# A squared-relu attention with a gated two-layer product behind it: shared PSUM pairs, av in bursts of a quad, visits of three items

## The chip, the cores and the metric

The kernel runs on one NeuronCore of a Trainium2 chip. The engines that matter are TensorE (PE in the profile; its weight loads are PEld), VectorE (DVE), ScalarE (ACT), GpSimd (POOL) and SyncE (SP, whose queue here issues DMAs). Each engine takes its instructions in the order in which the program lists them, and waits on semaphores for others. The metric is the device time of one execution in microseconds; the kernel before took 425.79 us (median of 3 runs, 425.36 to 425.98).

## The reference

Eight batches, 12 heads, 448 positions, 64 values a head. Attention without softmax: the scores are cut at zero and squared. The heads' outputs, side by side, are 3584 tokens of 768 values, which go through a 768 x 2048 product, a sigmoid-gated activation and a 2048 x 768 product.

```python
def _attn_ref(q, k, v):
    S = q.shape[2]
    scores = (1.0 / np.sqrt(q.shape[-1])) * np.matmul(q, k.transpose(0, 1, 3, 2))
    attn = np.maximum(scores, 0.0) ** 2 / S
    return np.matmul(attn, v)

def _moe_ref(x, w_in, w_out):
    h = x @ w_in
    g = h * (1.0 / (1.0 + np.exp(-1.702 * h)))
    return g @ w_out

x = attn_out.transpose(0, 2, 1, 3).reshape(B * S, H * D)
out = _moe_ref(x, w_in, w_out)
```

## The kernel before

**Attention.** The work unit is a quad: four heads of one batch, so three quads a batch and 24 in all (`units`, number u). A quad's 448 positions are cut into J = 7 slots of 64 keys. For a slot, `scores` (L145) runs four 64x64 matmuls side by side in the array, each 448 wide, into one PSUM pair `sc` (two banks). `relu2` then makes `rl` from it with a relu (ACT, L159; for slot 3 of the quads of batch 1 DVE, L156) and squares it on DVE into `at` (L160). `av_mm` (L170) multiplies a slot's `at` with v and adds it to the quad's PSUM pair `av` over the seven slots. `xt_evac` (L187) copies a finished `av` on DVE into `xt`, the transposed tokens of a group.

**The two products.** The tokens are cut into NG = 8 groups of 6 or 8 blocks of 64, so 384 or 512 tokens by turns. `m1(g, f)` (L226) makes 128 of the 2048 middle values for a group: six matmuls into the PSUM tile `ht`, then gelu on ACT (L231, `gf`), then scaling to fp16 on POOL (L233, `gt`). One such call is called an ht group here. `m2(g, m, h)` (L244) makes half of the output columns for 128 tokens: 16 matmuls into `op`, an eviction by DVE (L249, `osb`), and with the second half two stores on SP (L255). This is an op group. `ht`, `op` and the PE transposes `tr` share one pool of two PSUM tiles, `ps_m`.

**PSUM and buffers.** `ps_s` has two pairs for `sc`, `ps_v` one pair for `av`. There are three `rl`, six `at` and five v buffers.

**The order.** It is written out by hand. `visit(n)` takes the next n slots: it issues their scores, then the av of the slots that earlier visits left in `pend` (up to the end of a quad), the xt copy where a quad is finished, and last the relus and squares of the new slots. Batch 0 runs alone in visits of two; PE transposes (`trans_pe`, L128, copied out by ACT at L133 or DVE at L135) make kT and qT for quads 0 to 5. Then the 16 ht groups of group 0 run, with visits for batch 1 between them. Quads 6 and up are loaded in fp32 by SP (`load_qk`, L80), cast by DVE (k) and POOL (q) at L102, and transposed by DMA on SP's queue (`trans`, L109). Their first loads stand in SP's queue behind `sp_gate` (L273), a tiny transfer that reads a w_out block and so waits for it. From group 1 on, a list `moe` mixes the ht groups of g with the op groups of g-1. Each adds its estimated time to `acc`, and when that passes a due time tv, a visit follows. If a group's first ht needs quads that aren't finished, visits are forced.

**Loads and weights.** POOL's queue issues the loads that cast to fp16: k, q (`load16`, L117) and v (`load_v`, L89), and the weights, w_in in four blocks of two transfers (`w1`, L262) and w_out in four blocks (`w2`, L267). Two w_in blocks are triggered at the start, the others and w_out from `pool_work`, each behind the ht group of that number, and so behind that group's `gt` in POOL's queue.

Of the kernel before, what the change touches and what calls it, by code (L numbers as in the profile page):

```python
# [15 lines left out]
def kernel(  # L16
# [9 lines left out]
    nc = tc.nc  # L26
# [26 lines left out]
    atp = ctx.enter_context(tc.tile_pool(name="atp", bufs=6))  # L53
# [4 lines left out]
    ps_s = ctx.enter_context(tc.tile_pool(name="ps_s", bufs=2, space=bass.MemoryType.PSUM))  # L58
    ps_v = ctx.enter_context(tc.tile_pool(name="ps_v", bufs=1, space=bass.MemoryType.PSUM))
# [133 lines left out]
    slots = [(u, j) for u in range(NU) for j in range(J)]  # L193
    pend = []
# [3 lines left out]
    def visit(n):  # L198
        new = slots[pos[0]:pos[0] + n]
        pos[0] += len(new)  # L200
        scs = [scores(u, j) for u, j in new]
        ready = []
        while pend:
            ready.append(pend.pop(0))
            if ready[-1][1] == J - 1:
                break
        for u, j, at in ready:
            av_mm(u, j, at)
        if ready and ready[-1][1] == J - 1:
            xt_evac(ready[-1][0])  # L210
            done_units[0] = ready[-1][0] + 1
        for (u, j), sc in zip(new, scs):
            pend.append((u, j, relu2(u, j, sc)))
# [23 lines left out]

    def m2(g, m, h):
        if h == 0:
            osb[g, m] = osp.tile([128, DM], F32, name="osb", tag="osb")  # L240
        ot = osb[g, m]
        op = ps_m.tile([128, 512], F32, name="op", tag="mm")
        for f in range(NF):
            nc.tensor.matmul(  # L244
                out=op[:, 0:NOUT],
                lhsT=gts[g][:, f, m * 128:(m + 1) * 128],
                rhs=wout[h][f // WO][:, f % WO, :],
                start=(f == 0), stop=(f == NF - 1))
        nc.vector.tensor_scalar(out=ot[:, h * NOUT:(h + 1) * NOUT], in0=op[:, 0:NOUT],  # L249
                                scalar1=1.0 / SC, scalar2=None, op0=ALU.mult)  # L250
        if h == 1:
            for i in range(2):
                b, j = divmod(gcum[g] + 2 * m + i, J)
                r0 = b * S + j
                nc.sync.dma_start(out=out[r0:r0 + 63 * J + 1:J, :],  # L255
                                  in_=ot[64 * i:64 * i + 64, :])
# [34 lines left out]
    with tc.manual_schedule():  # L291
# [20 lines left out]
        trans_pe(0, "q", 4)  # L312
        n = 0
        while pos[0] < NP * J:
# [5 lines left out]
            if n == 5:  # L320
                trans_pe(2, "k", 0)
                trans_pe(2, "q", J)
            if n == 9:
                load16(4, "k")
                load16(4, "q")
            if n == 10:
# [18 lines left out]
        while pend:  # L345
            visit(0)
# [20 lines left out]
        def step_visit(n):  # L367
            visit(n)
            if pos[0] < len(slots):
                u = slots[pos[0]][0]  # L370
# [72 lines left out]
```

## Time and profile before

| | |
|---|---|
| timed runs | 425.79 us (425.36 to 425.98) |
| profiled execution | 424.03 us, its span 422.3 us |
| granted TensorE clock | 0.991 (mean) |
| busy in the span | TensorE 93%, ACT 49%, DVE 45%, POOL 31% |
| loads on POOL's queue | k 6, q 6 and v 24 of 224 KB; w_in 8 of 384 KB; w_out 4 of 768 KB (sizes as they land) |
| loads and stores on SP's queue | k 18 and q 18 of 448 KB; 56 stores of 192 KB |

The span is that of the profiled execution, from its first instruction to its last; the execution's own time is a little more. A row of the chain or the timeline reads: start, duration, engine, line, operation, output<-input, count, and in brackets the idle time before it with what ended it. A row of waits reads: who waited <- for whom: us in total, times, the longest. A row of the stage table gives the length of a stage, the busy time of each engine with its number of instructions, the granted clock, the share of 16 DMA engines that was asked for, and GB/s. A row of DMA issues ends with KB each and the median us to landing, or with the latter alone.

### The profile page before, as it was taken

What the parts mean: (1) busy time and instruction counts of PE and PEld (TensorE: products, weight loads), DVE (VectorE), ACT (ScalarE), POOL (GpSimd) and SP (SyncE); (2) the same over time, 40 slices, a digit from 0 to 9 for tenths busy, and PEclk for the clock granted to TensorE, in tenths of its full rate; (3) what the DMA queues carried; (4) which work ended last, traced back from release to release, by engine and by line L of the source; (5) the groups of instructions that cost most, each with busy time, mean ns of one, the idle gap of its engine ahead of it and who ended that gap; (6) DMA issues with size and microseconds to landing.
All of it is one profiled execution on the core that took longest, in us unless ns stands there. A gap on an engine that the chain in (4) does not pass through costs nothing.

```text
span 422.3 us, 7800 instructions
## 1 busy us (share of the span) xinstructions
PE 392.4 (93%) x3176; PEld 198.5 (47%) x3176; DVE 189.7 (45%) x292; ACT 208.8 (49%) x298; POOL 129.5 (31%) x200
## 2 busy tenths in 40 slices
PE   3868989699999999999999999999989999999994
PEld 1433445234345555444445555444445555555562
DVE  0885672236556353466346464554345443110121
ACT  4875761257765553666455553665455563222100
POOL 8304653505232322144133133144122211223100
PEclk9999999979999999999999999999999999999999
DMA  8986999967979199438446298467131211111122
GB/s 124 201 132 86 151 177 254 244 159 182 211 125 207 35 187 189 126 63 194 127 78 151 66 191 189 126 79 178 39 74 33 58 39 37 40 37 40 37 76 75
DMA packets 64900, 50.85 MB, mean 120 GB/s; under 512 B 35680, under 2 KB 61280, under 8 KB 64864
## 3 DMA queue, kind: packets, MB, share of 16 engines
q1 hardware_dynamic: 47712, 35.79, 35.5%
q0 software_dynamic: 17152, 14.55, 23.3%
q8 instruction: 25, 0.41, 0.4%
q14 instruction: 11, 0.09, 0.1%
HBM read 45.61 MB, written 11.01 MB: 134 GB/s over the span
## 4 chain that ended last, share of the span: by engine, by line
PE 78%; DVE 8%; ACT 6%; issue 3%; DMA 3%; POOL 1%; ACTq 0%; POOLq 0%
PE op L244 34%; PE ht L226 31%; PE sc L145 7%; PE av L170 6%; ACT rl L159 5%; DVE at L160 3%; DVE xt L187 2%; DMA qT<-q 2%; DMA q<-in_q_dram 1%; PE tr L128 1%; ACT gf L231 1%; DVE k L102 1%; DVE qT L135 0%; POOL gt L233 0%; DVE osb L249 0%
## 5 line engine op out<-in xcount | busy, mean ns | idle before, releaser
L159 ACT ACTIVATE rl<-sc 128x896 f16<-128x896 f32 x165 | 141.8, 920 | 62.7 <-PE sc L145 62.1
L226 PE MATMUL ht<-xt,win 128*128 128x384 f16 (+1 forms) x768 | 161.4, 355 | 2.5 <-DVE xt L187 2.5
L160 DVE TENSOR_TENSOR at<-rl 128x896 f16<-128x896 f16 x168 | 111.8, 679 | 93.3 <-ACT rl L159 93.1
L233 POOL TENSOR_SCALAR gt<-gf 128x384 f16<-128x384 f32 (+1 forms) x128 | 76.1, 595 | 252.9 <-ACT gf L231 251.6
L244 PE MATMUL op<-wout,gt 128*128 128x384 f16 x896 | 153.3, 326 | 0.0
L231 ACT ACTIVATE gf<-ht 128x384 f32<-128x384 f32 (+1 forms) x128 | 69.8, 546 | 117.9 <-PE ht L226 92.3
L244 PEld LDWEIGHTS <-gt 128*128 128x128 f16 x896 | 86.3, 98 | 63.4 <-issue 5.6
L226 PEld LDWEIGHTS <-win 128*128 128x128 f16 x768 | 70.3, 98 | 82.5 <-issue 24.8
L249 DVE TENSOR_SCALAR osb<-op 128x384 f32<-128x384 f32 x56 | 31.2, 557 | 116.1 <-PE op L244 116.1
L145 PE MATMUL sc<-qT,kT 64*64 64x448 f16 x672 | 53.0, 375 | 12.2 <-ACT rl L159 5.1
L170 PE MATMUL av<-at,v 64*64 64x448 f16 x672 | 50.9, 359 | 4.2 <-DVE at L160 3.2
L145 PEld LDWEIGHTS <-kT 64*64 64x64 f16 x672 | 15.4, 106 | 43.8 <-issue 37.4
L170 PEld LDWEIGHTS <-v 64*64 64x64 f16 x672 | 22.0, 108 | 20.7 <-issue 11.0
L187 DVE CAST xt<-av 128x768 f16<-128x768 f32 (+2 forms) x36 | 26.9, 774 | 7.5 <-PE av L170 7.3
L89 POOL DMA_DIRECT2D v<-in_v_dram x24 | 18.0, 751 | 2.1 <-PE ht L226 1.0
L102 POOL CAST q<-qst 128x896 f16<-128x896 f32 x18 | 16.9, 939 | 5.1 <-DMA qst<-in_q_dram 4.9
L102 DVE CAST k<-kst 128x896 f16<-128x896 f32 x18 | 15.4, 856 | 1.1 <-DMA kst<-in_k_dram 1.1
L128 PE MATMUL tr<-ident,k 128*64 128x128 f16 x84 | 4.2, 253 | 5.2 <-DMA k<-in_k_dram 5.2
L128 PEld LDWEIGHTS <-k 128*64 128x64 f16 x84 | 3.1, 129 | 6.8 <-DMA k<-in_k_dram 5.2
L135 DVE COPY qT<-tr 128x896 f16<-128x896 f16 (+1 forms) x5 | 2.8, 568 | 7.2 <-ACT qT L133 7.0
L262 POOL DMA_DIRECT2D win<-in_moe_w_in_dram x8 | 5.5, 692 | 1.0 <-DMA v<-in_v_dram 0.5
L117 POOL DMA_DIRECT2D k<-in_k_dram x6 | 4.6, 764 | 1.8 <-DMA v<-in_v_dram 0.9
(17 smaller groups left out, 27.0 us busy)
## 6 DMA issues: line engine op xcount, KB each, us to landing
out_dram<-osb SPq DMA_DIRECT2D x56, 192.0 KB, 2.8
kst<-in_k_dram SPq DMA_DIRECT2D x18, 448.0 KB, 5.1
qst<-in_q_dram SPq DMA_DIRECT2D x18, 448.0 KB, 5.9
v<-in_v_dram POOLq DMA_DIRECT2D x24, 224.0 KB, 5.2
win<-in_moe_w_in_dram POOLq DMA_DIRECT2D x8, 384.0 KB, 7.9
wout<-in_moe_w_out_dram POOLq DMA_DIRECT2D x4, 768.0 KB, 12.8
k<-in_k_dram POOLq DMA_DIRECT2D x6, 224.0 KB, 5.4
q<-in_q_dram POOLq DMA_DIRECT2D x6, 224.0 KB, 5.9
```

Source lines behind the costliest of these rows:

```text
L89: nc.gpsimd.dma_start(out=x, in_=quad(v, b, pr))
L102: eng.tensor_copy(out=o, in_=i)
L145: nc.tensor.matmul(out=sc[c, a, 0:S], lhsT=st["kT"][r, j, c], rhs=st["qT"][r, :, c], start=True, stop=True)
L159: nc.scalar.activation(out=rl, in_=sc[:, :, 0:S], func=AF.Relu)
L160: nc.vector.tensor_tensor(out=at, in0=rl, in1=rl, op=ALU.mult)
L170: nc.tensor.matmul(out=st["av"][64 * a:64 * a + 64, s, 0:S], lhsT=st["v16"][r, a, 64 * j:64 * j + 64], rhs=at[r, a, :], start=(j == 0), st ...
L187: nc.vector.tensor_copy(out=xts[g][:, 2 * pr:2 * pr + 2, 64 * (lo - gcum[g]):64 * (hi - gcum[g])], in_=av[:, :, 64 * (lo - b * J):64 * (hi ...
L226: nc.tensor.matmul(out=ht[:, 0:n], lhsT=w[:, kk, fo:fo + 128], rhs=xts[g][:, kk, 0:n], start=(kk == 0), stop=(kk == NK - 1))
L231: nc.scalar.activation(out=gf[:, 0:n], in_=ht[:, 0:n], func=AF.Gelu_apprx_sigmoid, scale=1.0 / SC)
L233: nc.gpsimd.tensor_scalar(out=gts[g][:, f, 0:n], in0=gf[:, 0:n], scalar1=SC, scalar2=1.0, op0=ALU.mult, op1=ALU.mult)
L244: nc.tensor.matmul(out=op[:, 0:NOUT], lhsT=gts[g][:, f, m * 128:(m + 1) * 128], rhs=wout[h][f // WO][:, f % WO, :], start=(f == 0), stop=( ...
L249: nc.vector.tensor_scalar(out=ot[:, h * NOUT:(h + 1) * NOUT], in0=op[:, 0:NOUT], scalar1=1.0 / SC, scalar2=None, op0=ALU.mult)
```

## The change

- The pool `ps_v` goes, and `ps_s` gets three pairs, which `sc` and `av` take in turn.
- The av of a quad no longer follows slot by slot. It is one item of its own in a new list `items`, 28 matmuls in a burst, placed behind the first two scores of the next quad (for the last quads of batch 1 and of the whole, at their own end). `at` gets ten buffers instead of six.
- Visits take one item in batch 0, and three behind it, with new due times (4.2 and 2.6 us for 3.1 and 1.9). In batch 0's loop the two first scores of quad 3 are issued ahead of quad 2's av.
- The loads of quads 4 and 5 and the third and fourth w_in block are triggered in batch 0's loop; the w_out blocks behind ht groups 1, 2, 4 and 5 instead of 7 to 10. The q copy of quad 2 moves from ACT to DVE.
- The last op group is done in two halves of 192 columns, and the last tile's stores leave in pieces, from SP and ACT at once.

The diff, cut to its core:

```diff
-    atp = ctx.enter_context(tc.tile_pool(name="atp", bufs=6))
+    atp = ctx.enter_context(tc.tile_pool(name="atp", bufs=10))
-    ps_s = ctx.enter_context(tc.tile_pool(name="ps_s", bufs=2, space=bass.MemoryType.PSUM))
-    ps_v = ctx.enter_context(tc.tile_pool(name="ps_v", bufs=1, space=bass.MemoryType.PSUM))
+    ps_s = ctx.enter_context(tc.tile_pool(name="ps_s", bufs=3, space=bass.MemoryType.PSUM))
...
-            st["av"] = ps_v.tile([128, 2, 512], F32, name="av", tag="av")
+            st["av"] = ps_s.tile([128, 2, 512], F32, name="av", tag="sc")
...
+    items = []
+    for u in range(NU):
+        late = u > 0 and u != 2 * NP
+        items += [("s", u, 0), ("s", u, 1)]
+        if late:
+            items.append(("v", u - 1, 0))
+        items += [("s", u, j) for j in range(2, J)]
+        if u == 2 * NP - 1 or u == NU - 1:
+            items.append(("v", u, 0))
...
     def visit(n):
-        new = slots[pos[0]:pos[0] + n]
+        new = items[pos[0]:pos[0] + n]
+        if new and ("v", new[-1][1], 0) == new[-1] and ("s", new[-1][1], J - 1) in new:
+            new.pop()
         pos[0] += len(new)
-        scs = [scores(u, j) for u, j in new]
-        ready = []
...
+        for t, u, j in new:
+            if t == "s":
+                made.append(scores(u, j))
+            else:
+                for jj in range(J):
+                    av_mm(u, jj, ats.pop((u, jj)))
+                made.append(None)
+        for (t, u, j), sc in zip(new, made):
+            if t == "s":
+                ats[u, j] = relu2(u, j, sc)
+            else:
+                xt_evac(u)
+                done_units[0] = u + 1
...
+    def store(g, m, lo, hi, engs):
+        for i in range(2):
+            b, j = divmod(gcum[g] + 2 * m + i, J)
+            r0 = b * S + j
+            engs[i].dma_start(out=out[r0:r0 + 63 * J + 1:J, lo:hi],
+                              in_=osb[g, m][64 * i:64 * i + 64, lo:hi])
...
+        last = g == NG - 1 and m == gblk[g] // 2 - 1
+        for part in range(2 if last and h == 1 else 1):
+            w = NOUT // 2 if last and h == 1 else NOUT
...
+            if last:
+                store(g, m, lo, lo + w, (nc.sync, nc.scalar))
+        if h == 1 and not last:
+            store(g, m, 0, DM, (nc.sync, nc.sync))
...
-            visit(min(2, NP * J - pos[0]))
+        while pos[0] < b0:
+            visit(1)
             n += 1
-            if n == 2:
+            if n == 4:
                 trans_pe(1, "k", 0)
                 trans_pe(1, "q", 0)
-            if n == 9:
                 load16(4, "k")
                 load16(4, "q")
+                load_v(4)
+                w1(2)
+            if n == 11:
+                trans_pe(2, "k", 0)
+                trans_pe(2, "q", 0)
+                load16(5, "k")
+                load16(5, "q")
+                load_v(5)
+            if n == 19:
                 trans_pe(3, "k", 0)
                 trans_pe(3, "q", 0)
-        visit(0)
+                w1(3)
+        visit(3)
...
-        pool_work = {0: lambda: load_v(4), 1: lambda: w1(2),
-                     3: lambda: (load16(5, "k"), load16(5, "q")), 4: lambda: load_v(5),
-                     5: lambda: w1(3), 7: lambda: w2(0, 0), 8: lambda: w2(0, 1),
-                     9: lambda: w2(1, 0), 10: lambda: w2(1, 1)}
+        pool_work = {1: lambda: w2(0, 0), 2: lambda: w2(0, 1),
+                     4: lambda: w2(1, 0), 5: lambda: w2(1, 1)}
...
-            if f in (4, 9):
+            if f in (2, 8):
...
-            if f % 4 != 3:
-                visit(min(2, 2 * NP * J - pos[0]))
+            if f % 2 == 1 or f > 12:
+                visit(min(3, b1 - pos[0]))
...
-            moe.append((x, 1000.0 if i < 4 else 1.9))
+            moe.append((x, 1000.0 if i < 3 else 2.6))
...
-                moe.append((x, 3.1))
+                moe.append((x, 4.2))
```

How instructions move, at three places. First POOL's queue around the last w_in block (win) and the w_out blocks (wout, named by column half), before:

```order
L233 TENSOR_SCALAR gt<-gf 128x384
L262 DMA win_103<-in_moe_w_in_dram 64x6x512 x2
L233 TENSOR_SCALAR gt<-gf 128x384 x2
L267 DMA wout_0_104<-in_moe_w_out_dram 128x8x384
L233 TENSOR_SCALAR gt<-gf 128x384
L267 DMA wout_1_105<-in_moe_w_out_dram 128x8x384
L233 TENSOR_SCALAR gt<-gf 128x384
L267 DMA wout_0_106<-in_moe_w_out_dram 128x8x384
L233 TENSOR_SCALAR gt<-gf 128x384
L267 DMA wout_1_107<-in_moe_w_out_dram 128x8x384
```

and now, from the last load ahead of group 0's first gelu output (gt) on:

```order
L88 DMA v_379<-in_v_dram 128x2x448
L283 DMA win_100<-in_moe_w_in_dram 64x6x512 x2
L245 TENSOR_SCALAR gt<-gf 128x384 x2
L288 DMA wout_0_101<-in_moe_w_out_dram 128x8x384
L245 TENSOR_SCALAR gt<-gf 128x384
L288 DMA wout_1_102<-in_moe_w_out_dram 128x8x384
L245 TENSOR_SCALAR gt<-gf 128x384 x2
L288 DMA wout_0_103<-in_moe_w_out_dram 128x8x384
L245 TENSOR_SCALAR gt<-gf 128x384
L288 DMA wout_1_104<-in_moe_w_out_dram 128x8x384
```

The last w_in block stood behind six of group 0's outputs and now stands ahead of all of them; the second w_out block, which SP's gate reads, stood behind the ninth and now stands behind the third.

Second, DVE's queue from quad 1's xt to quad 2's (the xt of a batch 0 quad is two casts), before:

```order
L187 CAST xt<-av 128x2x384
L187 CAST xt<-av 128x2x64
L160 TENSOR_TENSOR at<-rl 128x896 x6
L135 COPY kT<-tr 128x896
L135 COPY qT<-tr 128x896
L160 TENSOR_TENSOR at<-rl 128x896
L187 CAST xt<-av 128x2x384
L187 CAST xt<-av 128x2x64
```

and now:

```order
L186 CAST xt<-av 128x2x384
L186 CAST xt<-av 128x2x64
L159 TENSOR_TENSOR at<-rl 128x896
L134 COPY kT<-tr 128x896
L134 COPY qT<-tr 128x896
L159 TENSOR_TENSOR at<-rl 128x896 x6
L186 CAST xt<-av 128x2x384
L186 CAST xt<-av 128x2x64
```

The copies of quad 3's kT and qT stand five squares earlier; the last two squares ahead of the second xt are now of quad 3.

Third, ACT's queue in group 2, where gf is the gelu of an ht group and rl a relu, before:

```order
L231 ACTIVATE gf<-ht 128x384 x2
L159 ACTIVATE rl<-sc 128x896 x4
L231 ACTIVATE gf<-ht 128x384 x2
L159 ACTIVATE rl<-sc 128x896 x2
L231 ACTIVATE gf<-ht 128x384 x2
L159 ACTIVATE rl<-sc 128x896 x2
```

and now:

```order
L243 ACTIVATE gf<-ht 128x384 x2
L158 ACTIVATE rl<-sc 128x896 x3
L243 ACTIVATE gf<-ht 128x384 x2
L158 ACTIVATE rl<-sc 128x896 x2
L243 ACTIVATE gf<-ht 128x384 x2
L158 ACTIVATE rl<-sc 128x896 x3
```

Three relus of one visit now stand in a row ahead of a gelu; the four that stood in a row before belong to two visits with an op group between them.

More of the change, by code (lines that the diff above doesn't have):

```diff
@@ L191, in xt_evac @@
         units[u] = None
-    slots = [(u, j) for u in range(NU) for j in range(J)]
-    pend = []
+    items = []
[7 more added lines that the diff above has]
+            items.append(("v", u, 0))
+    ats = {}
     pos = [0]
@@ L241, in m2 @@
         ot = osb[g, m]
[L242 to L256, printed above, removed]
+        last = g == NG - 1 and m == gblk[g] // 2 - 1
+        for part in range(2 if last and h == 1 else 1):
+            w = NOUT // 2 if last and h == 1 else NOUT
+            op = ps_m.tile([128, 512], F32, name="op", tag="mm")
+            for f in range(NF):
+                nc.tensor.matmul(
+                    out=op[:, 0:w],
+                    lhsT=gts[g][:, f, m * 128:(m + 1) * 128],
+                    rhs=wout[h][f // WO][:, f % WO, part * w:(part + 1) * w],
+                    start=(f == 0), stop=(f == NF - 1))
+            lo = h * NOUT + part * w
+            nc.vector.tensor_scalar(out=ot[:, lo:lo + w], in0=op[:, 0:w],
+                                    scalar1=1.0 / SC, scalar2=None, op0=ALU.mult)
+            if last:
+                store(g, m, lo, lo + w, (nc.sync, nc.scalar))
+        if h == 1 and not last:
+            store(g, m, 0, DM, (nc.sync, nc.sync))
     w_rows = moe_w_in.rearrange("(a kk d) f -> a d kk f", a=2, d=D)
@@ L404 @@
                 acc += T2
-            while acc >= tv and (pos[0] < len(slots) or pend):
-                if pos[0] < len(slots):
-                    if slots[min(pos[0] + 1, len(slots) - 1)][0] // NP + 1 - 3 < m1_done:
-                        step_visit(2)
-                else:
-                    visit(0)
-                acc -= tv
+            while acc >= tv and pos[0] < len(items):
+                if all(t == "s" or u // NP - 2 < m1_done for t, u, j in items[pos[0]:pos[0] + 3]):
+                    step_visit(3)
+                    acc -= tv
+                else:
+                    acc = tv - 0.01
 _INS = ['q', 'k', 'v', 'moe_w_in', 'moe_w_out']
```

36 lines of the change are left out of this document (10 added, 26 removed).

## The prediction

> **What bounds the kernel now.** I read the first part of the page, then the busy time of each engine by stage, then what TensorE (PE) waits for, and last the chain of waits and the timeline at the places where it stands.
>
> ```profile
> span 422.3 us, 7800 instructions
> PE 392.4 (93%) x3176; PEld 198.5 (47%) x3176; DVE 189.7 (45%) x292; ACT 208.8 (49%) x298; POOL 129.5 (31%) x200
> core 0: us, PE busy (x) PEld busy (x) DVE busy (x) ACT busy (x) POOL busy (x), PEclk, DMA share, GB/s
> 8.28:31.69 23.41, 17.59 (x252) 8.68 (x252) 17.62 (x30) 18.40 (x22) 6.38 (x10) 1.00 1.04 166
> 31.69:66.13 34.44, 30.70 (x324) 14.93 (x321) 22.55 (x33) 21.79 (x33) 17.69 (x27) 1.00 0.98 144
> 66.13:90.10 23.97, 19.56 (x110) 9.03 (x107) 5.07 (x8) 6.59 (x11) 9.02 (x13) 0.86 1.19 261
> 90.10:123.88 33.78, 32.18 (x273) 14.56 (x270) 20.19 (x32) 23.09 (x32) 11.71 (x16) 1.00 0.65 154
> 123.88:359.80 235.92, 233.32 (x1881) 118.64 (x1881) 115.49 (x174) 126.42 (x183) 67.66 (x104) 1.00 0.52 112
> PE sc L145 <- DMA qT<-q: 4.4, 1, 4.4
> PE ht L226 <- DVE xt L187: 2.5, 6, 0.7
> ```
>
> TensorE is the bound from 90 us on: in the long stage it is busy 233.32 of 235.92 us, so a gain there must come off TensorE's own work. Ahead of 90 us it isn't. In batch 0 (to 31.69) it stands 5.8 us while DVE and ACT make a relu and a square of every score pair. In the next stage (group 0's ht beside batch 1) it stands 3.7 us, and in the third 4.4 us, with a granted clock of 0.86. The idle time in front and the mode changes between attention and the two products behind are what can be won.
>
> **Batch 0.** The rows that price it:
>
> ```profile
> 9.87 0.63 DVE L160 TENSOR_TENSOR at<-rl 128x896 f16<-128x896 f16 x1 [1.64 <-ACT rl L159]
> 19.96 5.77 ACT L159 ACTIVATE rl<-sc 128x896 f16<-128x896 f32 x7
> 24.45 1.16 DVE L187 CAST xt<-av 128x768 f16<-128x768 f32 x2 [0.48 <-PE av L170]
> 25.52 2.28 DVE L160 TENSOR_TENSOR at<-rl 128x896 f16<-128x896 f16 x4
> 29.73 0.53 DVE kT L135
> 31.38 0.38 PE L170 MATMUL av<-at,v 64*64 64x448 f16 x4 [1.21 <-DVE at L160]
> 32.82 0.49 PE L226 MATMUL ht<-xt,win 128*128 128x384 f16 x2 [0.30 <-DVE xt L187]
> ```
>
> The first ht group ends at 32.82 + 0.49 = 33.31, held by the xt of quad 2 on DVE. In the new order DVE does, from 9.87 to the end of that xt: 23 squares (two of batch 1 now go first), 6 copies (quad 2's q comes over from ACT) and three xt pairs. Back to back that is 23 x 0.57 (2.28 / 4) + 6 x 0.53 + 3 x 1.16 = 19.8, so 29.7 us at the earliest. The first nine squares come at ACT's pace of 0.82 (5.77 / 7) instead. Following the two queues through the three PSUM pairs by hand, DVE loses some 1.2 us ahead of the first xt and nothing after the second: 30.9, and the ht group ends 0.4 later, at 31.3. Gain 2.0 (3.2 without any gap; nothing if DVE keeps the idle time that it shows), with two score pairs of batch 1 already done.
>
> **ht of group 0.** 14 more ht groups lie between there and the three op groups that begin at 66.3, in both orders. TensorE enters attention 8 times instead of 12, and has two score pairs fewer to do. What an entry costs:
>
> ```profile
> 226.47 2.71 PE op L244 x16
> 230.15 0.50 PE sc L145 x8
> 230.66 0.38 PE av L170 x8
> 232.12 2.60 PE op L244 x16
> ```
>
> Eight sc behind a big product take 0.12 more than eight av, and 16 op behind av take 0.11 more than 16 op behind ht: 0.23 for each attention block. A score pair is 0.19. So 4 x 0.23 + 2 x 0.19 = 1.3 off. Of the 3.7 us of standing I find 2.7 again: an ht group now follows at once on the PE transposes of quads 4 and 5 and wants the PSUM buffer that their copies hold, which stand behind up to three squares on DVE (about 1 us each time), and the last av burst waits for its last square (0.7). That makes 1.3 + 1.0 = 2.3 of gain; from 1.0 lost (the copies more than twice as late) to 5.0. The op groups then begin 4.3 earlier, at 62.0.
>
> **Quad 6.** The largest single term.
>
> ```profile
> 64.33 0.62 SPq L273 DMA_DIRECT2D gate<-wout  x1
> 66.30 7.80 PE op L244 x48
> 76.08 1.33 SPq L109 DMA_TRANSPOSE kT<-k  x1
> 77.52 7.32 DMA qT<-q
> 84.97 0.96 PE sc L145 x7
> 85.94 2.67 PE ht L226 x6
> 88.61 0.89 PE sc L145 x8
> 89.50 0.67 PE av L170 x8
> 197.79 1.40 PE ht L226 x6
> 390.94 2.59 PE ht L226 x12
> qT<-q SPq DMA_TRANSPOSE x10, 3.0
> qT<-q SPq DMA_TRANSPOSE x3, 4.7
> L102 DVE CAST k<-kst 128x896 f16<-128x896 f32 x18 | 15.4, 856 | 1.1 <-DMA kst<-in_k_dram 1.1
> ```
>
> The loads of quads 6 to 8 wait on SP behind the gate, until the second w_out block has landed at 64.33. With the last weights they then fill the DMA engines (share 1.19 in that stage), and quad 6's q transpose lands 7.32 us after issue; the median is 3.0 from 170 to 350 us and 4.7 from 130 to 170. TensorE stands 4.4, and then runs on a lower clock: sc 0.96 and 0.89 for 0.50, ht 2.67 for 1.40, av 0.67 for 0.38, which is 0.46 + 0.39 + 1.27 + 0.29 = 2.4 more. Together 6.8.
>
> Now all w_in blocks and quads 4 and 5 are triggered inside batch 0, and the w_out blocks behind the 2nd, 3rd, 5th and 6th gelu output of group 0. By the sizes in the table ahead, 8.9 MB land ahead of the gate, which at the 166 to 200 GB/s that DMA moves there opens it at about 50. What remains is a short chain. The k cast stands on DVE behind the third op's eviction (0.56) in either order, so it ends at 62.0 + 7.8 + 0.6 + 0.9 = 71.3; behind k's transpose issue of 1.3, q's starts at 72.7 and lands at 75.7 (3.0) or 77.4 (4.7). TensorE arrives at 62.0 + 7.8 + 4 x 1.3 = 75.0 (four ht groups ahead of the scores, where five stood). A stall of 0.7 to 2.4; I take 1.3, nearer the quiet rows. The 1.21 us in which TensorE stood up to 31.38 left the clock at 1.00 in that stage, so I charge none. Gain 6.8 - 1.3 = 5.5 (nothing, if the transpose is as late behind the op groups as now).
>
> The Trainium skill ("TensorE: Matmul & The Clock Gate", Part 1: The HAM clock gate) puts the fall to half clock behind an idle window of about 3.4 us. By it 2.4 would still keep the clock and the 4.4 lost it, which the clock of 0.86 in that stage bears out.
>
> In the stage behind (90.10 to 123.88) TensorE stands 1.6. One block fewer and the third PSUM pair take something of it; a visit of three scores that comes one ht behind another waits 0.4 for its third pair: gain 0.5 (0.5 lost to 1.8).
>
> **Groups 2 to 6.** 39 attention blocks instead of 51: 12 x 0.23 = 2.8 off. In no group does the first ht still follow closely on its batch's last av, so the 2.5 us behind xt go. Against that stands ACT's order:
>
> ```profile
> 235.08 1.73 ACT L159 ACTIVATE rl<-sc 128x896 f16<-128x896 f32 x2 [2.34 <-PE sc L145]
> 235.53 2.12 PE L226 MATMUL ht<-xt,win 128*128 128x384 f16 x12
> 236.77 0.49 ACT L231 ACTIVATE gf<-ht 128x384 f32<-128x384 f32 x1
> ```
>
> Two ht groups end at 237.65 here, and the first one's gelu at 237.26: 0.39 to spare before a third product wants its PSUM buffer, of which there are two. With three scores and no av in that place ht ends 0.19 earlier (+0.19 for a score pair, -0.38 for two av), and the third relu puts the gelu 0.82 later. TensorE then stops for 0.82 + 0.19 - 0.39 = 0.62. The pattern (three scores, two 384-wide ht groups, an op) stands 7 times in the new order: 4.3 lost. A 512-wide pair of ht gives 0.6 more cover, which just does; an op between gives 2.6, an av burst 1.3. Net gain 2.8 + 2.5 - 4.3 = 1.0; 5.3 if none stops, 3.3 lost at twice as many.
>
> **The end.**
>
> ```profile
> 416.96 0.56 DVE L249 TENSOR_SCALAR osb<-op 128x384 f32<-128x384 f32 x1 [2.04 <-PE op L244]
> 417.55 1.11 SPq L255 DMA_DIRECT2D out_dram<-osb  x2
> L244 PEld LDWEIGHTS <-gt 128*128 128x128 f16 x896 | 86.3, 98 | 63.4 <-issue 5.6
> ```
>
> The last eviction is half as wide (0.28 less), and its two stores leave from SP and ACT at once instead of one 0.56 behind the other: 0.84. The 16 more weight loads cost from nothing to 1.6 (16 x 98 ns); nearly all loads run beside matmuls now, but behind shorter ones, so 0.3. Gain 0.5 (0.8 lost to 0.8).
>
> The Trainium skill ("DMA: Bandwidth & Descriptors", Anatomy of one DMA) gives a transfer on GpSimd's path 2.0 us fixed and 436 GB/s beside, so by estimate 0.34 less for 48 KB than for 192 KB, if SP's path is alike. By it the total would be 0.3 lower; no run here shows so small a store.
>
> **The sum**: 2.0 + 2.3 + 5.5 + 0.5 + 1.0 + 0.5 = 11.8. The profiled execution took 424.03, so 412.2; the median of the timed runs, 425.79, is 1.76 above it, so **414.0**.
>
> **The rivals.** (1) *The front stays as long as it is.* DVE has no less to do in batch 0 than before, and copies still stand between its squares; if its work decides and not its order, the 2.0 and 2.3 go: 418.3. For it: 17.62 of 23.41 us busy, with one copy and two squares more to come. Against: stops like the 1.21 us behind a square, which more square buffers and a burst that starts later can cover. (2) *Quad 6 is late anyway.* If q's transpose takes 7.32 again it lands at 80.0, the stall is 5.0, and the 2.4 of slow clock return: 7.4 instead of 1.3, so 420.1. For it: three v loads are triggered just ahead of it. Against: they are 0.7 MB, where 261 GB/s over 24 us (6.3 MB) moved before. (3) *Slower: every visit of three scores stops TensorE.* There are 35; if ACT, with three relus in a row, comes late to the first gelu behind each, the other 28 cost 0.62 too, 17.4 more: 431.4. It decides from 19 such visits on (11.8 / 0.62). For it: that only 0.39 is spare. Against: ACT is busy 126.42 of 235.92, and behind each of the 28 an op, an av burst or a wider ht covers. (4) *No difference*: parts of all three eat the gain.
>
> **How the numbers follow.** My forecast 0.58, with its own range of 410 to 418; rival 1 0.13, rival 2 0.15, rival 3 0.09, rival 4 0.05. The first three are faster by over 0.2% (0.85 us, about what a measurement can tell from no change): 0.86. The fourth is the 0.05, the third rival the 0.09. The range of 8 in 10 takes in rivals 1 and 2 and leaves out 3, 4 and the lower tail: 409.5 to 420.5.
>
> **What would show it.** The first ht group ends near 31.3 and the three op groups start near 62; the gate is issued near 50 instead of 64.33; q's transpose of quad 6 lands within 3 to 5 us, TensorE waits 0.5 to 2.5 for it, and the clock stays at 1.00 there; ht waits no more for xt; some 7 waits of op for ACT's gelu, of about 0.6, are new. I am wrong if those waits sum to over 10 us, if the clock falls again behind the op groups, or if the first ht group still ends at 33.

## The result and the profile after

The changed kernel took **412.89 us** (median of 4, 412.28 to 414.31) against 425.88 us (425.36 to 426.15) for the kernel before beside it: a ratio of 0.9701, 95% interval 0.9674 to 0.9728. That is 13.0 us less, inside the predicted range and 1.1 below the predicted 414.0. The profiled execution took 412.28 us with a span of 410.5, so the span fell by 11.8. The other 1.2 us lie in the profiled executions: before's lay 1.85 below its median, this one 0.6 below its own.

The first part of the page of the changed kernel, and the busy time of each engine by stage. The cuts are the first score, the end of the first ht group, the start of the three op groups, the first score of quad 6, the first ht of group 2, and then 349 us.

```profile
span 410.5 us, 7828 instructions
PE 382.3 (93%) x3192; PEld 200.7 (49%) x3192; DVE 189.7 (46%) x294; ACT 205.7 (50%) x297; POOL 131.6 (32%) x200
core 0: us, PE busy (x) PEld busy (x) DVE busy (x) ACT busy (x) POOL busy (x), PEclk, DMA share, GB/s
8.77:32.14 23.37, 16.89 (x268) 9.37 (x267) 19.79 (x35) 19.48 (x23) 11.38 (x17) 1.00 1.24 199
32.14:62.39 30.25, 27.01 (x308) 14.07 (x307) 19.87 (x29) 19.84 (x31) 12.04 (x19) 1.00 1.24 242
62.39:76.01 13.62, 12.98 (x73) 6.88 (x72) 2.79 (x6) 2.83 (x5) 6.37 (x9) 1.00 0.64 115
76.01:111.96 35.95, 34.88 (x312) 16.10 (x312) 23.56 (x36) 26.59 (x38) 15.73 (x20) 1.00 0.92 199
111.96:349.00 237.04, 231.34 (x1877) 120.42 (x1874) 114.77 (x171) 124.45 (x182) 68.56 (x104) 1.00 0.50 109
```

The prediction's stages of the kernel before were cut elsewhere: the second cut stood at the start of the first ht group, the fourth behind quad 6's first block, the fifth inside the first ht group of group 2. At the cuts used here the first three stages before were:

```profile
8.28:33.31 25.03, 18.91 (x262) 9.26 (x265) 18.78 (x32) 18.40 (x22) 6.38 (x10) 1.00 0.97 156
33.31:66.30 32.99, 29.55 (x316) 14.46 (x317) 21.56 (x31) 21.79 (x33) 17.69 (x27) 1.00 1.03 151
66.30:84.97 18.67, 14.27 (x78) 7.45 (x77) 3.64 (x6) 3.48 (x6) 8.41 (x12) 0.95 1.19 253
```

TensorE's busy time fell from 392.4 to 382.3, though the products and the attention are the same. A part of that is fewer mode changes, another the full clock behind the op groups: TensorE stood 4.4 us in the third stage, with slow matmuls behind it (a clock of 0.86 up to 90.10), and now stands 0.6, at a clock of 1.00 there and in the stage behind. A third part is av: a matmul counts as busy until its modelled end, so short waits between slots stand in this time, and it shrinks where av runs in a burst: eight av took 0.82 at 26.28 before, 28 take 1.52 at 28.51 now. The 84 av of batch 0 take 4.55 us of busy time for 8.32, those beside group 0's ht 4.87 for 6.96. In the long last stage, however, TensorE now stands 5.7 of 237.04 us, where it stood 3.1 of 237.28 (from 122.52, the first ht of group 2, to 359.80). The waits of TensorE name why:

```profile
PE op L266 <- ACT gf L243: 4.1, 7, 0.6
...
PE ht L238 <- DVE kT L134: 2.1, 2, 1.6
...
PE ht L238 <- DVE osb L272: 1.5, 2, 1.2
...
PE ht L238 <- DVE xt L186: 0.9, 1, 0.9
...
PE tr L127 <- ACT gf L243: 0.7, 2, 0.4
...
PE sc L144 <- DMA qT<-q: 0.6, 1, 0.6
```

Against before, ht's 2.5 us for xt have shrunk to 0.9, one wait at the first ht group, and the 4.4 for quad 6's transpose to 0.6. New are seven waits of op for ACT's gelu, as predicted, and 1.5 us of ht for an op's eviction `osb`, which I had not foreseen. The timeline shows the four places:

```profile
49.26 0.61 SPq L294 DMA_DIRECT2D gate<-wout  x1
...
72.86 1.22 SPq L108 DMA_TRANSPOSE qT<-q  x1
...
76.01 0.76 PE L144 MATMUL sc<-qT,kT 64*64 64x448 f16 x12 [0.64 <-DMA qT<-q]
...
111.27 0.76 PE L144 MATMUL sc<-qT,kT 64*64 64x448 f16 x12
111.96 2.12 PE L238 MATMUL ht<-xt,win 128*128 128x384 f16 x12
114.67 2.76 PE L266 MATMUL op<-wout,gt 128*128 128x384 f16 x16 [0.58 <-ACT gf L243]
...
128.09 3.08 DVE L159 TENSOR_TENSOR at<-rl 128x896 f16<-128x896 f16 x3 [2.78 <-ACT rl L158]
131.10 0.61 DVE L101 CAST k<-kst 128x896 f16<-128x896 f32 x1
131.64 0.54 DVE L272 TENSOR_SCALAR osb<-op 128x384 f32<-128x384 f32 x1
132.23 1.14 PE L238 MATMUL ht<-xt,win 128*128 128x384 f16 x6 [1.19 <-DVE osb L272]
```

The gate is issued at 49.26 instead of 64.33, and q's transpose lands by 75.87. At 111.27 stands the pattern of the prediction (three scores, two 384-wide ht groups, an op), and the op stops for 0.58. At 132.23 an ht group wants the PSUM tile that the last op left, but its eviction stands on DVE behind three squares and a k cast.

The end, in the timeline and in the DMA issues of the last 11 us (queue, operation, count, KB each, median us from issue to landing):

```profile
406.34 0.36 DVE L272 TENSOR_SCALAR osb<-op 128x192 f32<-128x192 f32 x1 [0.96 <-PE op L266]
```

```profile
out_dram<-osb SPq DMA_DIRECT2D x2, 48.0 KB, 1.9
out_dram<-osb ACTq DMA_DIRECT2D x2, 48.0 KB, 2.1
```

From the last matmul's end to the span's end it is 4.2 us now and was 5.4.

### The profile page after: what moved, and what is told of

Its sections match the earlier page's. It is cut to its first block, busy times and chain, and to the rows that moved or that the text cites. A ratio compares the mean times of both kernels' runs of the same rounds, so it can differ in the third digit from the quotient of the medians.

```text
span 410.5 us, 7828 instructions
## 1 busy us (share of the span) xinstructions
PE 382.3 (93%) x3192; PEld 200.7 (49%) x3192; DVE 189.7 (46%) x294; ACT 205.7 (50%) x297; POOL 131.6 (32%) x200
## 4 chain that ended last, share of the span: by engine, by line
PE 76%; ACT 9%; DVE 8%; issue 4%; DMA 2%; POOL 0%; ACTq 0%; DVEq 0%; POOLq 0%
PE op L266 35%; PE ht L238 27%; ACT rl L158 7%; PE av L169 7%; PE sc L144 6%; DVE at L159 4%; ACT gf L243 2%; DMA q<-in_q_dram 1%; DVE rl L155 1%; DMA qT<-q 1%; DVE xt L186 1%; DVE kT L134 1%; DVE qT L134 0%; DVE osb L272 0%; POOL gt L245 0%
## 5 line engine op out<-in xcount | busy, mean ns | idle before, releaser
L238 PE MATMUL ht<-xt,win 128*128 128x384 f16 (+1 forms) x768 | 158.8, 353 | 4.6 <-DVE kT L134 2.1
L266 PE MATMUL op<-wout,gt 128*128 128x384 f16 (+1 forms) x912 | 153.2, 323 | 4.1 <-ACT gf L243 4.1
L245 POOL TENSOR_SCALAR gt<-gf 128x384 f16<-128x384 f32 (+1 forms) x128 | 78.4, 612 | 239.3 <-ACT gf L243 237.5
L159 DVE TENSOR_TENSOR at<-rl 128x896 f16<-128x896 f16 x168 | 113.3, 687 | 78.4 <-ACT rl L158 78.2
L266 PEld LDWEIGHTS <-gt 128*128 128x128 f16 x912 | 88.0, 98 | 66.1 <-issue 8.8
L272 DVE TENSOR_SCALAR osb<-op 128x384 f32<-128x384 f32 (+1 forms) x57 | 31.2, 548 | 121.2 <-PE op L266 121.2
L144 PE MATMUL sc<-qT,kT 64*64 64x448 f16 x672 | 47.5, 363 | 6.9 <-DVE qT L134 3.6
L169 PE MATMUL av<-at,v 64*64 64x448 f16 x672 | 36.5, 351 | 1.9 <-ACT rl L158 1.5
L169 PEld LDWEIGHTS <-v 64*64 64x64 f16 x672 | 19.5, 107 | 15.7 <-issue 6.4
L127 PE MATMUL tr<-ident,q 128*64 128x128 f16 x84 | 4.2, 251 | 1.3 <-ACT gf L243 0.7
```

Source lines behind the costliest of these rows:

```text
L144: nc.tensor.matmul(out=sc[c, a, 0:S], lhsT=st["kT"][r, j, c], rhs=st["qT"][r, :, c], start=True, stop=True)
L159: nc.vector.tensor_tensor(out=at, in0=rl, in1=rl, op=ALU.mult)
L169: nc.tensor.matmul(out=st["av"][64 * a:64 * a + 64, s, 0:S], lhsT=st["v16"][r, a, 64 * j:64 * j + 64], rhs=at[r, a, :], start=(j == 0), st ...
L238: nc.tensor.matmul(out=ht[:, 0:n], lhsT=w[:, kk, fo:fo + 128], rhs=xts[g][:, kk, 0:n], start=(kk == 0), stop=(kk == NK - 1))
L245: nc.gpsimd.tensor_scalar(out=gts[g][:, f, 0:n], in0=gf[:, 0:n], scalar1=SC, scalar2=1.0, op0=ALU.mult, op1=ALU.mult)
L266: nc.tensor.matmul(out=op[:, 0:w], lhsT=gts[g][:, f, m * 128:(m + 1) * 128], rhs=wout[h][f // WO][:, f % WO, part * w:(part + 1) * w], sta ...
```

## The experiments

The theory was the prediction's own account: about half of the gain is quad 6, through the earlier triggers; the new stops behind ACT eat what the rarer mode changes bring in groups 2 to 6; batch 0 goes at DVE's pace; the end brings about one microsecond. The rivals: quad 6 would have been on time through the rest of the change as well, three-item visits are themselves the gain (or the loss), and batch 0 is set by something else than DVE. All ratios are to the kernel before on the same chip. The lines of code in the diffs are from the changed kernel, unless said otherwise.

### The triggers alone, taken away and added

The third and fourth w_in block go back behind ht groups 1 and 5, the w_out blocks behind 7 to 10:

```diff
-                w1(2)          # behind load_v(4) in batch 0
-                w1(3)          # behind trans_pe(3, "q", 0)
-        pool_work = {1: lambda: w2(0, 0), 2: lambda: w2(0, 1),
-                     4: lambda: w2(1, 0), 5: lambda: w2(1, 1)}
+        pool_work = {1: lambda: w1(2), 5: lambda: w1(3), 7: lambda: w2(0, 0), 8: lambda: w2(0, 1),
+                     9: lambda: w2(1, 0), 10: lambda: w2(1, 1)}
```

> The changed kernel with the third and fourth w_in block and the four w_out blocks triggered where the kernel before triggers them; all else stays changed. Theory: the gate opens again near 60, the loads of quads 6 to 8 and the last weights then share the DMA engines with quad 6's transposes, q's lands 6 us or more after issue, TensorE waits some 4.5 us and its clock falls for some microseconds (2.4): about 412.9 + 6.3 = 419. Rival (the gain is attention's own: PSUM pairs, bursts, longer visits): within 1 us of 412.9.

Measured: 418.61 us, ratio 0.9858 (0.9811 to 0.9904). Its waits of TensorE, its timeline of SP's queue, and the stretch from 75 to 80 us:

```profile
PE sc L144 <- DMA qT<-q: 5.0, 1, 5.0
PE op L266 <- ACT gf L243: 4.1, 7, 0.6
```

```profile
58.94 0.60 SPq L294 DMA_DIRECT2D gate<-wout  x1
...
73.08 4.44 SPq L108 DMA_TRANSPOSE qT<-q  x1
```

```profile
75.00:80.00 5.00, 0.09 (x4) 0.12 (x8) 0.00 (x0) 0.60 (x1) 2.90 (x4) 0.70 1.19 215
```

The gate comes 9.7 us later, q's transpose is issued at the same time as in the changed kernel (73.08 against 72.86) and yet occupies its queue for 4.44 instead of 1.22 and lands 6.7 us after issue instead of 3.0, while the DMA engines are asked for 1.19 of what they have. TensorE does nothing for 5.0 us, and the clock falls. So it isn't the order of SP's queue that made quad 6 late, but what the DMA engines carried at that moment. From the op groups to the first ht of group 2 it takes 54.6 us instead of 49.7.

The same two edits without the rest, in the kernel before:

```diff
+                w1(2)          # behind load16(4, "q") at n == 9
+                w1(3)          # behind trans_pe(3, "q", 0) at n == 10
-        pool_work = {0: lambda: load_v(4), 1: lambda: w1(2),
-                     3: lambda: (load16(5, "k"), load16(5, "q")), 4: lambda: load_v(5),
-                     5: lambda: w1(3), 7: lambda: w2(0, 0), 8: lambda: w2(0, 1),
-                     9: lambda: w2(1, 0), 10: lambda: w2(1, 1)}
+        pool_work = {0: lambda: load_v(4), 1: lambda: w2(0, 0), 2: lambda: w2(0, 1),
+                     3: lambda: (load16(5, "k"), load16(5, "q")),
+                     4: lambda: (load_v(5), w2(1, 0)), 5: lambda: w2(1, 1)}
```

> The kernel before with the weight triggers alone moved as in the change (w_in 3 and 4 in batch 0's loop, w_out behind ht groups 1, 2, 4 and 5). Theory: the wait of 4.4 for quad 6 falls to about 1 and the clock stays, so 6 us less: about 420. Rival: early triggers only help together with the earlier op groups; by themselves they take DMA time from batch 0's loads and give back half: 423 or more.

Measured: 418.02 us, ratio 0.9839 (0.9795 to 0.9882). Its chain of waits at that place:

```profile
67.76 7.80 PE op L244 x48
75.56 6.47 PE ht L226 x30
82.04 0.53 PE sc L145 x8
```

The op groups, five ht groups and quad 6's scores follow without a gap, and the scores run at full speed (eight in 0.53, where seven took 0.96). The stretch to group 2 is 6.2 us shorter than before (50.2 for 56.4). Batch 0 is 1.3 us longer in this profile, but its new wait, 1.1 us for a v load, ends at 12.52, and the first trigger that was moved is issued at 22.30, so it isn't the loss that the rival expected. The two experiments add up: the triggers alone are worth 1.61% of the time before (6.9 us), the rest alone 1.42% (6.0), both together 2.99%. Half of the gain is the triggers, and the rival that quad 6 would be on time without them has fallen.

### Visits of two instead of three

```diff
-            moe.append((x, 1000.0 if i < 3 else 2.6))
+            moe.append((x, 1000.0 if i < 3 else 1.73))
-                moe.append((x, 4.2))
+                moe.append((x, 2.8))
-                    step_visit(3)                # both places, and the check of pos[0]:pos[0] + 3
+                    step_visit(2)
```

> The changed kernel with visits of two items (due times 2.8 and 1.73) from group 1 on; bursts, shared pairs and early weights stay. 71 attention blocks in groups 1 to 6 instead of 49. Theory: 22 x 0.23 = 5.1 more for the entries; the seven waits of op for gelu (4.1) and one of 1.2 for an eviction go: 412.9 - 0.2, so 412 to 414. Rival A (entries cost nothing by themselves, and three relus in a row are the whole price of the long visits): 408. Rival B (an entry costs twice as much as it looks): 418.

Measured: 413.18 us, ratio 0.9721 (0.9682 to 0.9761), not to be told from the changed kernel's 0.9701. Its waits of TensorE:

```profile
PE sc L144 <- ACT rl L158: 2.9, 6, 0.6
...
PE ht L238 <- DVE osb L272: 0.5, 1, 0.5
...
PE op L266 <- ACT gf L243: 0.4, 1, 0.4
```

With 71 attention blocks instead of 49, six of the seven stops behind ACT's gelu go (4.1 to 0.4) and most of the wait for `osb` too. What the mode changes cost comes in their place: 22 blocks more at 0.23 make 5.1, against 3.7 and 1.0 of waits gone. Group 1 takes 37.58 us for 35.95 (four entries and two score pairs more), groups 2 to 6 268.93 for 270.90, together 0.3 less where the sum has 0.4 more. So with three items a visit instead of two, the rarer entries were no net gain as they stood. They became one once the stops were removed by other means:

### An op between the two ht groups

Where a visit of three scores would be followed by two 384-wide ht groups and an op, the op goes between the two, and no visit comes between it and the second ht group:

```diff
+                    three = all(t == "s" for t, u, j in items[pos[0]:pos[0] + 3])
                     step_visit(3)
+            nx = [x[0] for x in moe[n + 1:n + 4]]
+            if (three and [x[0] for x in nx] == ["m1", "m1", "m2"]
+                    and gblk[nx[0][1]] == 6 and nx[0][1] == nx[1][1]):
+                moe[n + 2], moe[n + 3] = moe[n + 3], moe[n + 2]
+                held = n + 2             # while acc >= tv ... and n != held
```

> The changed kernel where, behind a visit of three scores with two 384-wide ht groups and an op next, the op is put between the two ht groups, and the next visit waits for the second ht. Theory: the seven waits of op for gelu (0.58 to 0.59 each in the changed kernel's profile, 4.1 together) go and nothing takes their place, so 4 us less than the changed kernel: 0.9605 of the kernel before instead of 0.9701. Rival: ACT or DVE is late for the next buffer instead, and 1 us or less is gained.

Measured: 408.51 us, ratio 0.9618 (0.9588 to 0.9649). Its timeline of TensorE at such a place:

```profile
226.95 0.76 PE L144 MATMUL sc<-qT,kT 64*64 64x448 f16 x12
227.64 1.15 PE L238 MATMUL ht<-xt,win 128*128 128x384 f16 x6
228.63 2.76 PE L266 MATMUL op<-wout,gt 128*128 128x384 f16 x16
231.23 1.14 PE L238 MATMUL ht<-xt,win 128*128 128x384 f16 x6
```

No brackets: nothing is waited for. The waits of op for gelu are gone, and groups 2 to 6 take 265.89 us for 270.90. That is 5.0 for seven stops, 0.72 each, where their rows summed to 4.1 (0.59 each). The stops were real and on TensorE's path, and cost a little more than their rows show. A reason stands in the rows above: where nothing is waited for, the op begins 0.16 us ahead of the modelled end of the ht (228.63 against 227.64 + 1.15), and a stop loses that too, 0.75 in all.

### The transposes of quads 4 and 5 ahead of the visit

In the changed kernel these two follow ht groups 2 and 8, with an ht group directly behind, which wants their PSUM tile. Put behind ht groups 1 and 7 they stand ahead of a visit instead:

```diff
-            if f in (2, 8):
-                trans_pe(4 + f // 8, "k", 0)
-                trans_pe(4 + f // 8, "q", 0)
+            if f in (1, 7):
+                trans_pe(4 + f // 7, "k", 0)
+                trans_pe(4 + f // 7, "q", 0)
```

> The changed kernel with the PE transposes of quads 4 and 5 issued behind ht 1 and 7 of group 0, ahead of the visit that now precedes them, so that their copies stand ahead of that visit's squares on DVE. Theory: the waits of ht for the kT copy (1.6 and 0.5) and of the transposes for gelu (0.7) become one of some 0.6 each for gelu: 1.5 to 2 us less than the changed kernel in the stage of group 0's ht. Rival: the copies were not the cause and the wait returns as one for relus or squares: no gain.

Measured: 409.86 us, ratio 0.9656 (0.9627 to 0.9686). Its timeline of TensorE:

```profile
32.67 0.58 PE L127 MATMUL tr<-ident,k 128*64 128x128 f16 x14
33.32 0.58 PE L127 MATMUL tr<-ident,q 128*64 128x128 f16 x14
33.83 0.76 PE L144 MATMUL sc<-qT,kT 64*64 64x448 f16 x12
34.52 2.12 PE L238 MATMUL ht<-xt,win 128*128 128x384 f16 x12
```

Three scores now run while DVE makes the copies. The 2.1 us of ht for kT and the 0.7 of the transposes for a gelu are gone and nothing has come in their place in that stage: from the first ht group to the op groups it is 29.32 us for 32.26, or 2.9 less, more than the 1.5 to 2 expected. Behind the op groups 1.0 of it is lost again: the scores there wait 2.3 us for q's transposes, in two waits, where it was 0.6, and the stretch to group 2 takes 50.69 us for 49.74. By the ratios the run is 1.9 us faster than the changed kernel. That part of the prediction (ht of group 0) was right in its mechanism: the copies behind the squares were what stood in the way.

### Both together

> Both edits, the op between the ht groups and the transposes ahead of the visit. Theory: the gains add, 5.5 to 6 us less than the changed kernel, 0.956 of the kernel before. Rival: an earlier end of group 0 runs into the transposes of quad 6 and 1 to 2 us of it are lost there: 0.960.

The edits of the last two. Measured: **404.70 us** (median of 6, 403.76 to 406.91), ratio 0.9535 (0.9506 to 0.9564). Both gains are kept: added, the two ratios' distances from the changed kernel's would make 0.957, just above the interval. This beats both kernels. Neither op's waits for gelu nor ht's for kT stand among its waits of TensorE. What is left there of gelu and of late transposes is

```profile
PE sc L144 <- DMA qT<-q: 1.0, 2, 0.6
...
PE ht L238 <- ACT gf L243: 0.2, 1, 0.2
```

### The last tile unsplit

```diff
-        last = g == NG - 1 and m == gblk[g] // 2 - 1
+        last = False
```

> The changed kernel with the last op group whole and the last tile's two stores behind each other on SP, as before. Theory: 4.2 us from the last matmul to the end become 5.4, less 0.3 for the 16 more matmuls: 0.9 longer, 413.8. Rival: a store's fixed time hides the split: 412.9 within 0.3.

Measured: 415.44 us, ratio 0.9776 (0.9744 to 0.9809). The two longest pieces at the end of its chain of waits:

```profile
383.19 23.41 PE op L266 x144
406.62 0.56 DVE osb L272
```

The last nine op groups take 23.41 here and 23.45 with the 16 additional matmuls and weight loads: these cost nearly nothing. From the last matmul to the end it takes 5.3 us for 4.2. So the profile gives the split 1.1 us, near the expected 0.9. The timed difference is 3.2 us by the ratios, and I don't put it down to the split: three of the six executions ran at a mean granted clock of 0.988 and one, the profiled, at 1.000. That one took 413.70, where the changed kernel's only execution at 1.000 took 412.94: 0.8 apart, and only roughly, since the kernel before took 424.17 beside the one and 425.88 beside the other. Two more executions, at 0.995 and 0.997, took 415.35 and 414.93, so the rest of the timed difference stays open.

### What sets the pace of batch 0

The prediction had DVE's work there as the bound. First, quad 2's q copy back on ACT, which takes 0.5 us off DVE:

```diff
-                trans_pe(2, "q", 0)
+                trans_pe(2, "q", J)
```

> The changed kernel with quad 2's q copy on ACT again, as before. Theory (DVE's queue decides batch 0): DVE has 0.53 less to do, and from the first score to the end of the first ht group 0.5 us less passes. Rival (ACT's relus decide): 0.9 more passes, since ACT does the copy between two relus.

Measured: 413.29 us, ratio 0.9735 (0.9697 to 0.9774). In its profiled execution the clock was 0.63 from 14 to 18 us, and the first ht group began at 31.30 instead of 29.96. With the clock fallen, that says nothing of the copy. To keep the clock from deciding, TensorE was given more to do: the kernel with both improvements, in which batch 0's scores are each computed twice into the same place (additional work, with the same values), without and with the copy on ACT:

```diff
-        for s in range(2):
+        for s in range(2 if u >= NP else 4):
+            s = s % 2
```

> The kernel with both edits (op between, transposes first), where in batch 0 every score pair is computed twice into the same PSUM pair, the second time with the same values: TensorE has 84 more matmuls there, some 4 us. It tests what makes the clock fall in batch 0 in some executions. Theory: it falls where TensorE is busy too little of a stretch, so with the fillers the mean granted clock is 0.998 or more in every execution; DVE and ACT set the pace, so the median is 404 to 406. Rival A: the falls have another cause; the clock is below 0.996 in one execution of three as before. Rival B: TensorE's own time counts in batch 0, and 2 us or more are lost: 407 or more.

> The same with quad 2's q copy on ACT, now that the clock should be alike in both. Theory (DVE's queue decides batch 0): from the first score to the end of the first ht group 0.5 us less than in the run beside it. Rival (ACT's relus decide): 0.9 more.

Measured: 405.86 us, ratio 0.9537 (0.9522 to 0.9553), and 406.55, ratio 0.9545 (0.953 to 0.9561). The clock held in both profiles. From the first score to the first ht it took 22.48 us with the additional scores and 21.19 without, so TensorE is itself close to the pace there. The copy on ACT made it 0.5 longer again, 22.96. It was neither the 0.5 less of a DVE that sets the pace alone nor the 0.9 more of an ACT that does. In a batch 0 that has the additional scores, DVE alone doesn't set the pace. For the changed kernel without them it stays open.

### The changed kernel once more

> The changed kernel itself, on the chip of the two runs beside it. Expected: 0.970 of the kernel before, and among its executions some with a clock below 0.996, these the longer ones by 1 to 2 us.

Measured: 412.01 us (411.57 to 414.49), ratio 0.9693 (0.967 to 0.9717): the result comes out a second time. Four executions at a mean clock of 0.998 to 0.999 took 411.57 to 412.17 us, and two at 0.990 took 414.43 and 414.49. One of these two is the profiled one; what it shows is told below.

## Why the prediction was right, and where it was off

The time was right, and so was the account of where it goes, in most terms; in two of them (ht of group 0, groups 2 to 6) parts that were off cancelled. By the two profiled executions:

| term | predicted | measured |
|---|---|---|
| batch 0 (first ht group ends 33.31, now 32.14) | 2.0 | 1.2 |
| ht of group 0 (32.99, now 30.25) | 2.3 | 2.7 |
| quad 6 and group 1 (op groups to group 2: 56.2, now 49.6) | 5.5 + 0.5 | 6.6 |
| groups 2 to 6 (271.0, now 270.9) | 1.0 | 0.1 |
| the end (28.8, now 27.6) | 0.5 | 1.2 |
| sum | 11.8 | 11.8 |

- **Batch 0** was mis-sized, and it is the term that the clock disturbs most. 0.5 of the missing 0.8 is no matter of the change: the first score began at 8.77 here, at 8.28 before, and at 8.3 to 8.5 in the other runs. From the first score to the end of the first ht group it took 25.03 us before, and 23.4 to 23.6 in the profiled executions that leave this stretch alone and whose av bursts all took 1.52 us (the changed kernel, the late triggers, the transposes first, both together, the end unsplit): 1.5 to 1.7 of 2.0. Where the clock fell it took 25.4 (visits of two) and 25.6 (the changed kernel once more), and nothing was gained. With the op between it took 24.9; its first burst took 2.83 us, though its windows show a clock of 1.00. In these three the first ht group ended at 33.2 to 33.9, where the prediction had named 33 as a sign of being wrong, and rival 1 came true for its 2.0, though by slow matmuls and not by DVE's work. The step that failed for such executions is that the prediction went by the queues of DVE and ACT alone and put the clock in batch 0 at nothing. Its one sentence on the clock there ("The 1.21 us in which TensorE stood up to 31.38 left the clock at 1.00 in that stage, so I charge none") was said of quad 6's stall.
- **ht of group 0** came to 2.7 for 2.3, but not by the two parts that were added up, so the agreement is partly luck. By the rows of the two stages TensorE's standing fell only from 3.4 to 3.2 us, where 1.0 was charged, and its busy time fell by 2.5, where 1.3 was charged for entries and score pairs. The new stops behind the transposes were right in kind: 2.1 us of ht for kT and 0.7 of the transposes for gelu, with 0.4 of the last av burst 3.2 in all where I had 2.7. Moving the transposes took just these 2.8 away. The prediction had no term for what a burst does to av itself (4.87 us of busy time for 6.96); no run separates that from the entries. The ht groups between are 15, not 14; the sum doesn't use it.
- **Quad 6** was right step by step: the gate at 49.26 ("about 50"), q's transpose at 72.86 (72.7 forecast), landed in 3.0 (3.0 or 4.7 forecast), a stall of 0.64 (1.3 taken), the clock at 1.00. Rival 2, that it is late anyway, fell; taking the triggers back gave its stall to the tenth (5.0). That run came out 6.7 us later by its ratio, near the 7.4 - 1.3 = 6.1 by which rival 2 stood above the forecast, and 4.4 by the two spans (4.9 in the stage itself, and its first score began 0.45 earlier). The trace shows one reason for less: 1.1 us of scores' waits for a relu and a gelu vanish where TensorE is late and slow anyway.
- **Groups 2 to 6** hold a step that was missed. The seven stops came where and as charged (4.1 for 4.3), at every place of the pattern and at no other. Not in the sum were two waits of ht for the op's eviction (1.5), at places where three scores, an op and two ht groups follow one another. The rows that I read for the pattern ("three scores, two 384-wide ht groups, an op") were ACT's; I did not ask the same question of DVE, on which the visit's squares, a k cast and the eviction stand in one queue. Of the 2.5 of waits for xt 2.3 lay in these groups and went, and 0.9 of scores' waits for relus went too, which was not in the sum. Another 0.6 was gained because three score pairs had been done earlier. That leaves 2.0 for the 12 entries, where 2.8 was charged.
- **Rival 3**, that every visit of three stops TensorE, fell: seven of 35 did. Its seed was right, since each stop cost 0.59 by its row and 0.72 by its removal.
- **The end** brought more than the 0.5 charged. The additional weight loads that I charged with 0.3 cost 0.04, and the 48 KB stores landed in 1.9 to 2.1 us where 192 KB take 2.7. The Trainium skill ("DMA: Bandwidth & Descriptors", Anatomy of one DMA), by its 2.0 us and 436 GB/s, let me estimate 0.34 less for these; the trace has 0.6 to 0.8 less, about twice that, on SP's and ACT's queues and from two stores each.

## What to carry to other kernels

A load late on the critical path can be late because of what else the DMA engines carry at that moment; look at which transfers could have been triggered while the engines were free (before, their share was 0.00 from 30 to 34 us), since that alone was half of the gain here. When attention is gathered into fewer, larger visits, the relus and squares of a visit become a burst in an in-order queue, and the next small thing in that queue (a gelu, an eviction, a copy out of PSUM) holds TensorE up; count what covers each of them, on every engine that takes part, and put a long product between. Such waits are cheap to remove by moving one instruction group: two moves of this kind gave 1.7% more than the change itself.

## What the runs showed of the hardware

**The clock can stay low, or fall, without a long wait.** Two stretches of batch 0 and its first av burst, in the windows and the timeline of the changed kernel's first profile:

```profile
14.00:18.00 4.00, 3.04 (x68) 2.06 (x68) 3.63 (x7) 3.81 (x5) 1.63 (x4) 1.00 1.21 195
29.00:33.00 4.00, 3.13 (x36) 1.55 (x27) 2.43 (x5) 1.57 (x3) 1.43 (x3) 1.00 1.24 205
```

```profile
15.55 1.52 PE L169 MATMUL av<-at,v 64*64 64x448 f16 x28 [0.43 <-ACT rl L158]
```

And in those of the same kernel once more:

```profile
14.00:18.00 4.00, 3.51 (x42) 1.85 (x44) 3.22 (x7) 2.63 (x4) 1.94 (x3) 0.67 1.21 191
29.00:33.00 4.00, 3.46 (x32) 1.75 (x32) 2.98 (x6) 2.11 (x3) 2.03 (x3) 0.57 1.25 204
```

```profile
14.08 0.57 PE L144 MATMUL sc<-qT,kT 64*64 64x448 f16 x8 [1.28 <-DVE qT L134]
15.06 2.60 PE L169 MATMUL av<-at,v 64*64 64x448 f16 x28 [0.40 <-ACT rl L158]
```

The same program with nearly the same waits, and 28 matmuls take 1.52 or 2.60 us. From the first score on, no wait of TensorE in batch 0 is longer than 1.4 us. The waits of 4.4 us (before) and 5.0 (late triggers) did end with a fallen clock, and 0.64 did not, but these falls have no such wait ahead of them. The Trainium skill ("TensorE: Matmul & The Clock Gate", A second HAM failure mode: psum-queue depth-cycling) describes falls of this kind: where TensorE idles briefly but often, the clock goes down and up again. The windows above agree: 0.67 and 0.57, and in the same profile 1.00 between them, from 22 to 29 us.

TensorE was busy for 16.89 of 23.37 us in the stretch where the clock held. That such a share is near a bound, so that some executions fall on one side of it and some on the other, is a guess. For it: with batch 0's scores computed twice, none of nine executions had a mean clock below 0.997 (0.998 had been expected in all, and three missed it), where two of the changed kernel's ten stood at 0.990 and took 2.5 us more. Against it: of the same kernel without the additional scores only one of six stood at 0.990, too few to tell, and a mean can hide a slow start, as with the op between (mean 1.00, first burst 2.83 us). It doesn't pay here: the additional scores cost 1.3 us each time, and the ratio was 0.9537 with them and 0.9535 without.

**An entry into attention costs about 0.2 us** of TensorE: 0.23 by rows quoted in the prediction. The visits of two agree with that size: with 22 more entries (5.1) and 4.7 less of waits the sum has 0.4 more time, and 0.3 less was measured, which makes 0.20 an entry, or 0.23 where each stop that went is taken at its 0.72. The 12 entries that groups 2 to 6 lost were worth 0.17 each by their rows. The Trainium skill ("TensorEngine Tiling (Array Packing)", Key Properties) says that a change of tiling mode drains the array. The cost here fits that; no run separates the drain from the rest of an entry.
